# RWKV-5 attention and a tanh-shrink MLP on one core: the four loads of a w_in piece shared out over two queues by halves of partitions, with new costs in the planner

## The chip, the core and the metric

The kernel runs on one core of a Trainium2 chip. The core's engines work side by side, each through its own list of instructions in order: TensorE (PE; its weight loads are shown as PEld), VectorE (DVE), ScalarE (ACT), GpSimd (POOL) and SyncE (SP). SP and POOL here issue the DMAs; each is a queue of its own. The time is device microseconds per execution: 605.67 us in the median of three (603.26 to 606.02) before the change.

## What is computed

First a linear recurrence for 4 batches of 8 heads with 768 steps and 48 values per head, then an MLP over the 3072 tokens of 384 values that come out of it:

```python
for t in range(S):
    kt, vt, rt = (k[:, :, t], v[:, :, t], r[:, :, t])
    cur = np.einsum('bhd,bhe->bhde', u[None] * kt, vt)
    y[:, :, t] = np.einsum('bhd,bhde->bhe', rt, state + cur)
    state = w[None, :, :, None] * state + np.einsum('bhd,bhe->bhde', kt, vt)
x = y.transpose(0, 2, 1, 3).reshape(B * S, H * D)
h = x @ w_in                       # 384 x 2048
g = h - np.tanh(h)
return (g @ w_out).astype(np.float32)   # 2048 x 384
```

w_in and w_out arrive as float64, the rest as float32.

## The kernel before, in words

**The recurrence** is worked in 24 units of 64 steps for two batches each (`unit(n)`): batch half z = 0 lies in rows (partitions) 0 to 63, z = 1 in rows 64 to 127. A unit fetches r, k and v, each in two DMAs of 96 KB (`fetch`, line 750, all on SP), transposes r and k on PE (`turn`, line 763), forms levels, outputs and the state's update on PE (line 717), and leaves its result in `xt`. A third of the heads' rows goes through a tile `rest` and from there by six small DMAs on POOL, SBUF to SBUF, into rows 48 to 63 and 112 to 127 of `xt` (`fill`, line 876). Two units make one block of 256 tokens for the MLP.

**The MLP** takes a block and 256 columns of w_in at a time (`hidden`): `h` on PE (line 168), five activations on ACT (177 to 185), four operations on DVE (192 to 198), then `o` (line 206) or, in the last eight sixteenths, a scheme with seven products (line 257), for which POOL forms sums of g.

**The weights** come in 16 pieces, in the order of n: two of w_in, two of w_out, and so on. A piece is loaded as 64-bit words into a staging tile `st` and converted to float32 by five operations on DVE and two on ACT (`convert`, lines 137 to 143). A piece of w_out is one DMA to all 128 rows, on SP. A piece of w_in has four parts, because each head pair is padded to 64 rows: `parts[0]` goes to rows 0 to 47 (288 KB), `parts[1]` to rows 48 to 63 (96 KB), `parts[2]` to rows 64 to 111 (288 KB), `parts[3]` to rows 112 to 127 (96 KB). All are issued at line 123. Before the change SP issues parts 0 and 2 and POOL parts 1 and 3. The conversion waits for all four.

**The order of the instructions** is not written by hand. Every task is given to a planner (`Plan.add`) with its engine, a cost in us, what it waits for and, for a DMA, `data`, the time that it takes of a common channel. `Plan.forward` plays the tasks through; `Plan.order` shakes their due times at random, some thousands of times from a fixed seed, and keeps what is no worse. The order of the best play is the order in which the kernel's instructions are written, on each engine and each queue. `steps` counts PE instructions for code loading; LANDS, LANDED and SLOW are what a DMA takes to land; LANES limits the DMAs in flight of a queue to 8; a task marked `gated` (the weights) may not start over 45 us before it is due. In the planner before, a DMA from whatever queue waits only for the common channel:

```python
channel = max(channel, start + 1.2) + t.data
end = max(end + self.LANDS, channel + self.LANDED) + self.slow(start)
```

Of the kernel before, what the change touches and what calls it, by code (L numbers as in the profile page):

```python
# [33 lines left out]
AHEAD = 2  # L34
# [266 lines left out]
class Plan:  # L301
# [6 lines left out]

    HOP, NEAR_HOP, LANDS, LANDED, LANES, EARLY, SPARE, WARM, SLOW = 0.16, 0.06, 2.4, 1.6, 8, 45.0, 20.0, 6.0, (60.0, 3.0)
    AHEAD, BUSY = 0.05, 240.0  # L310
    CHUNK, CHUNK_0, ASKED, COMES, FIRST = 256, 192, 55, 3.4, 9.5
# [4 lines left out]

    def add(self, engine, cost, run, after=(), due=1e9, data=0, gated=False, steps=0):
        t = SimpleNamespace(engine=engine, cost=cost, run=run, after=[x for x in after if x], due=due, data=data,
                            gated=gated, steps=steps, then=[], n=len(self.tasks))
        for x in t.after:  # L320
            x.then.append(t)
        self.tasks.append(t)
        return t
# [12 lines left out]
    def forward(self, due, until=1e9):  # L336
# [3 lines left out]
        waiting = self.queues(ready, count)  # L340
        free, lanes, channel = dict(self.BEGIN), {}, 0.0
        step, bound, comes, fills = 0, self.CHUNK_0, 0.0, iter(self.fills)
# [3 lines left out]
        while len(done) < len(ready):  # L346
# [40 lines left out]
            if t.data:  # L387
                channel = max(channel, start + 1.2) + t.data
                end = max(end + self.LANDS, channel + self.LANDED) + self.slow(start)
                lanes[e] = lanes[e][1:] + [end]  # L390
# [58 lines left out]

    def order(self, first=2500, tries=500):  # L450


        due = [t.due for t in self.tasks]
        for t in reversed(self.tasks):
            for x in t.then:
                due[t.n] = min(due[t.n], due[x.n] - t.cost - self.HOP - (self.LANDS if t.data else 0))
        plan = self.forward(due)
        for _ in range(4):
            due = self.backward(plan)
            plan = self.forward(due)  # L460
        chance = Random(5)

        def moved():
            by, at, wide = chance.choice((0.3, 1, 2, 5)), chance.uniform(0, until), chance.choice((15, 40, 100, 700))
            return [x + chance.gauss(0, by) * (start is not None and abs(start - at) < wide / 2) for x, start in zip(due, plan[1])]


        until = self.BUSY
        plan = self.forward(due, until)
        for _ in range(first):  # L470
            new = moved()
            other = self.forward(new, until)
            if other[0] <= plan[0]:
                plan, due = other, new
        plan = self.forward(due)
        until = plan[0]
        for _ in range(tries):
            new = moved()
            other = self.forward(new)
            if chance.random() < .5:  # L480
                latest = self.backward(other)
                again = self.forward(latest)
                if again[0] < other[0]:
                    other, new = again, latest
            if other[0] <= plan[0]:
                plan, due = other, new
        self.due = due
        _, starts, done = plan
        self.forward(due)
        fitted, order = {n: (free, runs) for free, n, runs in self.fitted}, []  # L490
        for t in done:
            t.start = starts[t.n]
            free, runs = fitted.get(t.n, (0.0, [])) if t.engine == "PE" else (0.0, [])
            order += [SimpleNamespace(engine="PE", cost=0.0, start=free, run=run) for run in runs]
            order.append(t)
        return order
# [19 lines left out]
def near(ctx, tc, r, k, v, w, u, out, shared, moe_w_in, moe_w_out):  # L516
# [136 lines left out]
    def fills(to):  # L653
# [20 lines left out]
    doubled = add("ACT", .6, lambda: A.copy(twice, inverse[:, :, None, 1:].to_broadcast([128, NP, 2, SHORT])), [now])  # L674
    now = tabled = add("PE", .7, table, [doubled], steps=8)
    downs = add("ACT", .5, lambda: A.copy(w_down, tab.rearrange("s (h d) -> s h d", h=H)[:, :, :D]), [now])
# [6 lines left out]
        out=ub.rearrange("p h d -> p (h d)"),  # L683
        in_=bass.AP(tensor=u.tensor, offset=u.offset, ap=[[0, 128], [1, H * D]])), data=.7)

# [15 lines left out]
    for n in range(weights.count):  # L701

        queues, data = (("SP",), (3.0,)) if n % 4 > 1 else (("SP", "POOL") * 2, (1.2, .95) * 2)
        of = [add(e, .55, lambda n=n, i=i, e=e: weights.load(n, i, e_of[e]), [converted[n - 4] if n >= 4 else None],
                  data=x, gated=True) for i, (e, x) in enumerate(zip(queues, data))]
        if weights.sources[n % 4 > 1].dtype != I64:
            converted.append(of[-1])
            continue
        step = steps(lambda n=n: weights.convert(n))
        now = of + ([converted[n - 2]] if n >= 2 else [])  # L710
        for name, cost in (("DVE", .47), ("DVE", .47), ("ACT", .84), ("ACT", .84), ("DVE", .87), ("DVE", .87), ("DVE", .87)):
            now = [add(name, cost, step, now)]
        converted += now
# [7 lines left out]
    def unit(n):  # L721
# [21 lines left out]
        direct = j == 0  # L743

        def fetch(name, src, after):
            def run(z):
                if name == "k" and not hasattr(t, "kt"):
                    t.kt = first_k[slot] if direct else load.tile([128, H, D], F32, name="kt", tag="kt")
                to = {"r": rt, "v": vt}.get(name)
                Q.dma_start(out=(t.kt if to is None else to)[HALF[z], :, :D],  # L750
                            in_=src[half * 2 + z, :, steps_at, :].rearrange("h t d -> t h d"))

            of = [add("SP", .65, lambda z=z: run(z), after, data=.71) for z in range(2)]
            return add("none", 0, lambda: None, of)
# [135 lines left out]
        if two:  # L890
            free = [b1.xt, b1.rest, b1.add, b1.cp, b1.diag]
        turns, turned = .46, 16
        x.turn = add("PE", turns, lambda: turn(rt, r_ps), [x.r] + free, steps=turned)
# [9 lines left out]
        if product:  # L903
            now = add("ACT", 1.05, own_k, [x.kT, w_us])
            x.own = add("PE", .7, own_levels, [now, x.rT, b2.out], steps=64)
            x.diag = add("DVE", .64, lambda: V.copy_predicated(t.at, same.bitcast(I32)[:, None, None, :].to_broadcast([128, 2, NP, SHORT]), own_lev), [x.own, b2.out])
# [7 lines left out]
        if two:  # L914
            now = add("PE", .66, from_state, both + [x.rT, b1.xt, b1.rest, b1.add, b2.decay, x.kT], steps=64)
            begun = [add("ACT", .15, between, [now])]
        x.lev = add("PE", .7 if two else (1.33 if swap else 1.73) if ch else .7, levels,
                    begun + [x.kT, x.rT, b2.out] + ([b2.decay, b1.xt, b1.rest, b1.add] if ch else []), steps=128 if ch and not two else 64)
        x.cp = add("DVE", .64, lambda: V.copy_predicated(t.at, before, lev), [x.lev, b2.out] + ([] if product else [x.diag]))  # L919
        x.out = now = add("PE", .95 if direct else 1.21, outputs,  # L920
                          [x.cp, x.diag, x.v, b1.xt, b1.rest, b1.add] + ([x.extra] if direct else [x.kw]), steps=96 if direct else 128)
        if direct:
            now = x.out = add("PE", .55, to_state, [now, x.kw], steps=64)
        x.xt = add("ACT", .96 if swap else .4, to_xt, [now, last_h.get(j - FIRST - 2) if slot == 0 else None])
        if not direct:
            x.rest = add("ACT", .62 if swap else .26, to_rest, [x.xt] + (filled.get((j - 2, "all"), []) if slot == 0 else []))
        x.add = add("DVE" if ch else "ACT", .47 if ch else 1.2, keep, [x.out, x.rest, x.xt]) if more else None
        x.decay = x.add if not ch else add("DVE", .47, lambda: V.tensor_tensor(state[:, :, :, :D], state[:, :, :, :D], w_all, ALU.mult), [x.add]) if more else None
        if direct:
            filled.setdefault((j, "all"), []).append(x.xt)  # L930
        elif slot == L - 1:
            filled[j, "all"] = [add("POOL", .52, lambda i=i, kk=kk: fill(i, kk), [x.rest, x.xt], data=.1)
                                for kk in range(NK) for i in range(2)]
# [17 lines left out]
    def finished_seven(t, x, half, due, pace):  # L951
# [9 lines left out]
        for i in (1, 0):  # L961
            now = steps[4 if i else 6]
            if t.fs[0]:
                now = add("DVE", .47, lambda i=i: dense.gather(t, i), [now], due + 3 * pace)
            stored[j, i] = [add("POOL", .6, lambda z=z, i=i: dense.store(t.os[i], L * j + i, z, G), [now], due + 4 * pace, data=.4)
                            for z in range(2)]

    def hidden(j, fs, f, due, pace, seven=False):
# [40 lines left out]
        for i in range(L):  # L1009
# [7 lines left out]
            if whole and j < d.NB - 1:  # L1017

                stored[j, i] = [add("POOL", .6, lambda z=z, i=i, ends=ends: dense.store(ends.o, L * j + i, z, G),
                                    [x.empty[-1]], due + 4 * pace, data=.4) for z in range(2)]  # L1020

# [339 lines left out]
```

## Time and profile before

| | |
|---|---|
| median of three | 605.67 us |
| the profiled execution, its own time | 607.26 us |
| its span, first to last instruction | 605.5 us |
| PE / PEld busy | 582.4 / 485.7 us (96% / 80%) |
| DVE / ACT / POOL busy | 466.4 / 403.3 / 201.0 us |
| w_in loads on SP | 16, 288 KB each, 5.5 us from issue to landing (median) |
| w_in loads on POOL | 16, 96 KB each, 6.0 us |
| w_out loads on SP | 8, 768 KB each, 4.5 us |
| r, k, v loads on SP | 140, 96 KB each, 2.9 to 3.4 us |
| fills of xt on POOL | 66, 16 KB each, 2.1 us |

The page's rows of 40 slices of 15 us each show busy tenths; DMA is the mean busy share of the 16 DMA engines:

```profile
PE   8877999999999999999999999999999999999996
DVE  6699699999999999867677776767765775555666
POOL 5002212021000123544455473425334435334540
DMA  6966585967300210110111020122201100100101
```

Nearly all of the DMA work lies in the first ten slices, where the weights are loaded and 16 of the 24 units run. PE's row has its low digits in the first four slices. Busy PE includes filler matmuls (line 655) that the planner sets into holes before the first real work. A profile is one execution; sums are made against its own time.

### The profile page before, as it was taken

To read this page: it belongs to the slowest core of one execution; us is meant where nothing else is said; L and a number is where in the kernel's file an instruction comes from. 1 tells how busy PE (TensorE), PEld (TensorE's weight loads), DVE (VectorE), ACT (ScalarE), POOL (GpSimd) and SP (SyncE) were. 2 spreads that over 40 slices of the span, in tenths; PEclk is the share of its full clock that TensorE was granted. 3 is DMA by queue.
4 is the path that set the end of the run, shared out by engine and by line. 5 is a ranking of instruction groups with operands and counts; after the bars stand their busy time and mean duration, and the time that the engine had idled before them with its cause. 6 is when DMAs were issued, how large, how long until landed. Compare 5 with 4: busy or idle time off the path is not lost.

```text
span 605.5 us, 14670 instructions
## 1 busy us (share of the span) xinstructions
PE 582.4 (96%) x5781; PEld 485.7 (80%) x5781; DVE 466.4 (77%) x782; ACT 403.3 (67%) x902; POOL 201.0 (33%) x366
## 2 busy tenths in 40 slices
PE   8877999999999999999999999999999999999996
PEld 4555767667777669999999999888889889889995
DVE  6699699999999999867677776767765775555666
ACT  3677699899866676655556686465866676565652
POOL 5002212021000123544455473425334435334540
PEclk9889899999999999999999999999999999999999
DMA  6966585967300210110111020122201100100101
GB/s 125 228 126 126 113 194 99 143 167 124 105 14 0 48 28 14 26 27 1 28 27 26 2 60 1 41 41 48 53 16 34 41 2 8 29 2 8 26 3 30
DMA packets 86326, 33.78 MB, mean 56 GB/s; under 512 B 78536, under 2 KB 80680, under 8 KB 86248
## 3 DMA queue, kind: packets, MB, share of 16 engines
q1 hardware_dynamic: 81084, 25.57, 21.1%
q0 software_dynamic: 4992, 6.99, 5.5%
q8 instruction: 47, 0.77, 0.5%
q14 instruction: 31, 0.25, 0.2%
q10 hardware_dynamic: 172, 0.20, 0.1%
HBM read 26.94 MB, written 4.72 MB: 52 GB/s over the span
## 4 chain that ended last, share of the span: by engine, by line
PE 76%; DVE 6%; DMA 5%; ACT 4%; issue 4%; SPq 3%; POOL 1%; DVEq 0%; ACTq 0%; POOLq 0%
PE h L168 37%; PE p L257 26%; PE o L206 6%; PE yk_ps L717 4%; SPq L750 3%; DMA st<-in_moe_w_in_dram 2%; DMA xt<-rest 1%; PE yk_ps L763 1%; POOL xt L876 1%; DMA st<-in_moe_w_out_dram 1%; DVE rT L767 1%; DVE at L919 1%; ACT s L177 1%; DVE tg L194 1%; DVE g L198 1%
## 5 line engine op out<-in xcount | busy, mean ns | idle before, releaser
L168 PE MATMUL h<-xt,w_in_sb 128*128 128x256 f32 x1152 | 285.7, 385 | 2.7 <-DMA xt<-rest 2.7
L168 PEld LDWEIGHTS h<-xt,w_in_sb 128*128 128x128 f32 x1152 | 214.6, 192 | 35.9 <-issue 2.1
L242 POOL TENSOR_TENSOR sg<-g 128x256 f32<-128x256 f32 x69 | 52.1, 755 | 176.7 <-DVE g L198 152.2
L257 PE MATMUL p<-mixed,sg 128*128 128x192 f32 x426 | 104.1, 326 | 0.0
L192 DVE TENSOR_TENSOR g<-h,th 128x512 f32<-128x512 f32 x96 | 65.8, 686 | 48.9 <-ACT s L177 23.0
L194 DVE SCALAR_TENSOR_TENSOR tg<-s,tg 128x512 f32<-128x512 f32 x96 | 71.1, 741 | 36.6 <-ACT tg L181 20.0
L181 ACT ACTIVATE tg<-h 128x512 f32<-128x512 f32 x96 | 57.2, 596 | 58.5 <-PE h L168 56.9
L179 ACT ACTIVATE th<-h 128x512 f32<-128x512 f32 x96 | 57.4, 598 | 39.1 <-PE h L168 39.0
L177 ACT ACTIVATE s<-h 128x512 f32<-128x512 f32 x96 | 57.4, 598 | 37.3 <-PE h L168 37.2
L876 POOL DMA_DIRECT2D xt<-rest x66 | 32.5, 499 | 146.3 <-ACT rest L855 145.8
L257 PEld LDWEIGHTS p<-mixed,sg 128*128 128x128 f32 x426 | 75.0, 190 | 0.3 <-issue 0.3
L198 DVE COPY_PREDICATED g<-small,tg 128x512 f32<-128x512 int32 x96 | 71.1, 741 | 4.7 <-DVE tg L196 0.5
L257 PE MATMUL p<-w_out_sb,g 128*128 128x192 f32 x284 | 71.9, 335 | 1.1 <-DVE at L919 1.1
L196 DVE SCALAR_TENSOR_TENSOR tg<-q,tg 128x512 f32<-128x512 f32 x96 | 67.5, 703 | 6.4 <-ACT q L183 2.4
L206 PE MATMUL o<-w_out_sb,g 128*128 128x384 f32 x192 | 71.3, 495 | 0.1
L183 ACT ACTIVATE q<-s,m1b 128x512 f32<-128x512 f32 x96 | 69.8, 727 | 0.6
L185 ACT ACTIVATE small<-s,smallb 128x512 f32<-128x512 f32 x96 | 69.6, 725 | 0.3
L257 PEld LDWEIGHTS p<-w_out_sb,g 128*128 128x128 f32 x284 | 51.8, 190 | 9.0 <-DVE at L919 1.5
L788 ACT ACTIVATE at<-same,du 128x64 f32<-128x64 f32 x184 | 47.9, 343 | 2.8 <-DVE du L784 2.6
L206 PEld LDWEIGHTS o<-w_out_sb,g 128*128 128x128 f32 x192 | 35.2, 190 | 15.8 <-DVE g L198 0.2
L246 POOL TENSOR_TENSOR sg<-sg,g 128x128 f32<-128x128 f32 x69 | 41.0, 594 | 5.1
L244 POOL TENSOR_TENSOR sg<-sg,g 128x128 f32<-128x128 f32 x69 | 36.6, 530 | 5.2
(133 smaller groups left out, 672.3 us busy)
## 6 DMA issues: line engine op xcount, KB each, us to landing
st<-in_moe_w_out_dram SPq DMA_DIRECT2D x8, 768.0 KB, 4.5
rt<-in_r_dram SPq DMA_DIRECT2D x48, 96.0 KB, 2.9
vt<-in_v_dram SPq DMA_DIRECT2D x48, 96.0 KB, 3.4
st<-in_moe_w_in_dram SPq DMA_DIRECT2D x16, 288.0 KB, 5.5
kt<-in_k_dram SPq DMA_DIRECT2D x44, 96.0 KB, 3.1
out_dram<-o POOLq DMA_DIRECT2D x44, 96.0 KB, 2.2
st<-in_moe_w_in_dram POOLq DMA_DIRECT2D x16, 96.0 KB, 6.0
xt<-rest POOLq DMA_DIRECT2D x66, 16.0 KB, 2.1
```

What stands on the lines that cost most here:

```text
L168: self.nc.tensor.matmul(t.h2[:, z], self.w_in_sb[:, t.f // 2, kk, z * 128 : (z + 1) * 128], self.xts[t.j][:, kk].rearrange("p b t -> p (b ...
L177: A.activation(out, t.h, AF.Square)
L179: A.activation(out, t.h, AF.Tanh)
L181: A.activation(out, t.h, AF.Tanh, scale=G1)
L183: A.activation(out, t.s, AF.Square, bias=self.m1b)
L185: A.activation(out, t.s, AF.Relu, bias=self.smallb, scale=-1.0)
L192: V.tensor_tensor(t.g, t.h, t.th, ALU.subtract)
L194: V.scalar_tensor_tensor(t.tg, t.s, C4, t.tg, ALU.mult, ALU.mult)
L196: V.scalar_tensor_tensor(t.tg, t.q, K1, t.tg, ALU.add, ALU.mult)
L198: V.copy_predicated(t.g, t.small.bitcast(I32), t.tg)
L206: self.nc.tensor.matmul(self.outs[i], t.g2[:, z, i * C : (i + 1) * C], self.w_out_sb[:, t.f + z, :], start=t.first and z == 0, stop=t.last ...
L257: self.nc.tensor.matmul(ps[bank][:, half * n : (half + 1) * n], a, b, start=t.first and half == 0, stop=t.last, skip_group_check=True)
```

## The change

Two things change. The parts of a w_in piece keep their order, but the queues become SP, POOL, POOL, SP: SP has rows 0 to 47 and then 112 to 127, POOL has rows 48 to 63 and then 64 to 111. And the planner gets a time for each half of the rows (`ports`), a line for each queue (`ring`), a `side` for each DMA that goes to one half, and new costs; its search starts four times from the same point and looks at the first 110 us at first, where it looked at 240.

```diff
-    HOP, NEAR_HOP, LANDS, LANDED, LANES, EARLY, SPARE, WARM, SLOW = 0.16, 0.06, 2.4, 1.6, 8, 45.0, 20.0, 6.0, (60.0, 3.0)
-    AHEAD, BUSY = 0.05, 240.0
+    HOP, NEAR_HOP, LANDS, LANDED, LANES, EARLY, SPARE, WARM, SLOW = 0.16, 0.06, 2.1, 1.35, 8, 45.0, 20.0, 6.0, (60.0, 1.5)
+    AHEAD, BUSY, STARTS = 0.05, 110.0, 4
+    HALF = 1.75
...
             if t.data:
-                channel = max(channel, start + 1.2) + t.data
-                end = max(end + self.LANDS, channel + self.LANDED) + self.slow(start)
+
+                begin = max(start + 1.4, ring.get(e, 0.0))
+                channel = max(channel, begin) + t.data
+                ring[e] = channel
+                if t.side is not None:
+                    ports[t.side] = max(ports[t.side], begin) + self.HALF * t.data
+                    ring[e] = max(channel, ports[t.side])
+                end = max(end + self.LANDS, ring[e] + self.LANDED) + self.slow(start)
...
-    def order(self, first=2500, tries=500):
+    def order(self, first=2000, tries=300):
...
-        queues, data = (("SP",), (3.0,)) if n % 4 > 1 else (("SP", "POOL") * 2, (1.2, .95) * 2)
+        queues, data, sides = (("SP",), (2.5,), (None,)) if n % 4 > 1 else (("SP", "POOL", "POOL", "SP"), (.82, .4, .82, .4), (0, 0, 1, 1))
...
-            of = [add("SP", .65, lambda z=z: run(z), after, data=.71) for z in range(2)]
+            of = [add(queue(z), .65, lambda z=z: run(z), after, data=.28, side=z) for z in range(2)]
...
-        turns, turned = .46, 16
+        turns, turned = .38, 16
...
-        x.lev = add("PE", .7 if two else (1.33 if swap else 1.73) if ch else .7, levels,
+        x.lev = add("PE", .6 if two else (1.06 if swap else 1.46) if ch else .56, levels,
...
-        x.out = now = add("PE", .95 if direct else 1.21, outputs,
+        x.out = now = add("PE", .86 if direct else .97, outputs,
...
-            filled[j, "all"] = [add("POOL", .52, lambda i=i, kk=kk: fill(i, kk), [x.rest, x.xt], data=.1)
+            filled[j, "all"] = [add("POOL", .52, lambda i=i, kk=kk: fill(i, kk), [x.rest, x.xt], data=.1, side=i)
```

The new `queue(z)` returns "SP" for both halves as it stands, so r, k and v stay on SP. The loop with four starts in `order` and some smaller costs of the same kind (the table's transposes, own levels, the first state, the loads of u, the stores of the output) are left out above. No operation of the kernel's own work is added or removed.

More of the change, by code (lines that the diff above doesn't have):

```diff
@@ L315, in __init__, with add @@
         self.tasks, self.fills = [], []
-    def add(self, engine, cost, run, after=(), due=1e9, data=0, gated=False, steps=0):
+    def add(self, engine, cost, run, after=(), due=1e9, data=0, gated=False, steps=0, side=None):
         t = SimpleNamespace(engine=engine, cost=cost, run=run, after=[x for x in after if x], due=due, data=data,
-                            gated=gated, steps=steps, then=[], n=len(self.tasks))
+                            gated=gated, steps=steps, side=side, then=[], n=len(self.tasks))
         for x in t.after:
@@ L340, in forward @@
         waiting = self.queues(ready, count)
-        free, lanes, channel = dict(self.BEGIN), {}, 0.0
+        free, lanes, channel, ring, ports = dict(self.BEGIN), {}, 0.0, {}, [0.0, 0.0]
         step, bound, comes, fills = 0, self.CHUNK_0, 0.0, iter(self.fills)
@@ L465, in moved @@
             return [x + chance.gauss(0, by) * (start is not None and abs(start - at) < wide / 2) for x, start in zip(due, plan[1])]
[L468 to L474, printed above, removed]
+        until, begun, best = self.BUSY, due, None
+        for _ in range(self.STARTS):
+            due = begun
+            plan = self.forward(due, until)
+            for _ in range(first):
+                new = moved()
+                other = self.forward(new, until)
+                if other[0] <= plan[0]:
+                    plan, due = other, new
+            if best is None or plan[0] < best[0]:
+                best = plan[0], due
+        due = best[1]
         plan = self.forward(due)
@@ L674, in near @@
     doubled = add("ACT", .6, lambda: A.copy(twice, inverse[:, :, None, 1:].to_broadcast([128, NP, 2, SHORT])), [now])
-    now = tabled = add("PE", .7, table, [doubled], steps=8)
+    now = tabled = add("PE", .5, table, [doubled], steps=8)
     downs = add("ACT", .5, lambda: A.copy(w_down, tab.rearrange("s (h d) -> s h d", h=H)[:, :, :D]), [now])
@@ L683, in near @@
         out=ub.rearrange("p h d -> p (h d)"),
-        in_=bass.AP(tensor=u.tensor, offset=u.offset, ap=[[0, 128], [1, H * D]])), data=.7)
+        in_=bass.AP(tensor=u.tensor, offset=u.offset, ap=[[0, 128], [1, H * D]])), data=.5)
     add("ACT", 1.3, lambda: A.activation(fixed("warm", [128, 1]), shared["one"], AF.Tanh), due=0)
@@ L701, in near @@
     for n in range(weights.count):
-        queues, data = (("SP",), (3.0,)) if n % 4 > 1 else (("SP", "POOL") * 2, (1.2, .95) * 2)
+        queues, data, sides = (("SP",), (2.5,), (None,)) if n % 4 > 1 else (("SP", "POOL", "POOL", "SP"), (.82, .4, .82, .4), (0, 0, 1, 1))
         of = [add(e, .55, lambda n=n, i=i, e=e: weights.load(n, i, e_of[e]), [converted[n - 4] if n >= 4 else None],
-                  data=x, gated=True) for i, (e, x) in enumerate(zip(queues, data))]
+                  data=x, gated=True, side=side) for i, (e, x, side) in enumerate(zip(queues, data, sides))]
         if weights.sources[n % 4 > 1].dtype != I64:
@@ L743, in unit, with queue @@
         direct = j == 0
+        def queue(z):
+            return "SP" if not z else "ACT" if n < 0 else "POOL" if n < 0 else "SP"
         def fetch(name, src, after):
@@ L749, in run @@
                 to = {"r": rt, "v": vt}.get(name)
-                Q.dma_start(out=(t.kt if to is None else to)[HALF[z], :, :D],
+                e_of[queue(z)].dma_start(out=(t.kt if to is None else to)[HALF[z], :, :D],
                             in_=src[half * 2 + z, :, steps_at, :].rearrange("h t d -> t h d"))
-            of = [add("SP", .65, lambda z=z: run(z), after, data=.71) for z in range(2)]
+            of = [add(queue(z), .65, lambda z=z: run(z), after, data=.28, side=z) for z in range(2)]
             return add("none", 0, lambda: None, of)
@@ L903, in unit @@
         if product:
-            now = add("ACT", 1.05, own_k, [x.kT, w_us])
-            x.own = add("PE", .7, own_levels, [now, x.rT, b2.out], steps=64)
+            now = add("ACT", 1.2, own_k, [x.kT, w_us])
+            x.own = add("PE", .5, own_levels, [now, x.rT, b2.out], steps=64)
             x.diag = add("DVE", .64, lambda: V.copy_predicated(t.at, same.bitcast(I32)[:, None, None, :].to_broadcast([128, 2, NP, SHORT]), own_lev), [x.own, b2.out])
@@ L914, in unit @@
         if two:
-            now = add("PE", .66, from_state, both + [x.rT, b1.xt, b1.rest, b1.add, b2.decay, x.kT], steps=64)
+            now = add("PE", .58, from_state, both + [x.rT, b1.xt, b1.rest, b1.add, b2.decay, x.kT], steps=64)
             begun = [add("ACT", .15, between, [now])]
-        x.lev = add("PE", .7 if two else (1.33 if swap else 1.73) if ch else .7, levels,
+        x.lev = add("PE", .6 if two else (1.06 if swap else 1.46) if ch else .56, levels,
                     begun + [x.kT, x.rT, b2.out] + ([b2.decay, b1.xt, b1.rest, b1.add] if ch else []), steps=128 if ch and not two else 64)
         x.cp = add("DVE", .64, lambda: V.copy_predicated(t.at, before, lev), [x.lev, b2.out] + ([] if product else [x.diag]))
-        x.out = now = add("PE", .95 if direct else 1.21, outputs,
+        x.out = now = add("PE", .86 if direct else .97, outputs,
                           [x.cp, x.diag, x.v, b1.xt, b1.rest, b1.add] + ([x.extra] if direct else [x.kw]), steps=96 if direct else 128)
         if direct:
-            now = x.out = add("PE", .55, to_state, [now, x.kw], steps=64)
+            now = x.out = add("PE", .5, to_state, [now, x.kw], steps=64)
         x.xt = add("ACT", .96 if swap else .4, to_xt, [now, last_h.get(j - FIRST - 2) if slot == 0 else None])
@@ L926, in unit @@
             x.rest = add("ACT", .62 if swap else .26, to_rest, [x.xt] + (filled.get((j - 2, "all"), []) if slot == 0 else []))
-        x.add = add("DVE" if ch else "ACT", .47 if ch else 1.2, keep, [x.out, x.rest, x.xt]) if more else None
+        x.add = add("DVE" if ch else "ACT", .47 if ch else .95, keep, [x.out, x.rest, x.xt]) if more else None
         x.decay = x.add if not ch else add("DVE", .47, lambda: V.tensor_tensor(state[:, :, :, :D], state[:, :, :, :D], w_all, ALU.mult), [x.add]) if more else None
@@ L964, in finished_seven @@
                 now = add("DVE", .47, lambda i=i: dense.gather(t, i), [now], due + 3 * pace)
-            stored[j, i] = [add("POOL", .6, lambda z=z, i=i: dense.store(t.os[i], L * j + i, z, G), [now], due + 4 * pace, data=.4)
+            stored[j, i] = [add("POOL", .6, lambda z=z, i=i: dense.store(t.os[i], L * j + i, z, G), [now], due + 4 * pace, data=.3)
                             for z in range(2)]
@@ L1019, in hidden @@
                 stored[j, i] = [add("POOL", .6, lambda z=z, i=i, ends=ends: dense.store(ends.o, L * j + i, z, G),
-                                    [x.empty[-1]], due + 4 * pace, data=.4) for z in range(2)]
+                                    [x.empty[-1]], due + 4 * pace, data=.3) for z in range(2)]
     for n in range(L * (FIRST + 2)):
```

## The prediction

> **What bounds the kernel now.** I read the table of stretches first, because the page's 96% for TensorE is an average. Columns: stretch, its length, busy us and count of PE, PE's weight loads, DVE, ACT, POOL, granted PE clock, DMA share, GB/s.
>
> ```profile
> 15.00:35.00 20.00, 17.05 (x267) 10.33 (x271) 14.54 (x25) 14.00 (x37) 0.57 (x1) 0.91 0.93 199
> 35.00:55.00 20.00, 15.56 (x365) 11.61 (x355) 19.77 (x36) 16.14 (x50) 3.94 (x8) 0.91 0.68 128
> 55.00:70.00 15.00, 11.96 (x178) 8.56 (x181) 9.73 (x18) 7.38 (x24) 0.76 (x2) 0.77 0.52 93
> 70.00:80.00 10.00, 10.00 (x229) 7.04 (x222) 9.20 (x18) 9.64 (x32) 3.52 (x7) 1.00 1.01 216
> 80.00:90.00 10.00, 9.19 (x169) 6.63 (x167) 9.11 (x16) 9.01 (x22) 2.98 (x6) 1.00 0.76 170
> 90.00:120.00 30.00, 28.12 (x564) 20.70 (x564) 28.58 (x50) 26.52 (x73) 4.93 (x10) 1.00 0.79 125
> 120.00:135.00 15.00, 13.80 (x189) 9.29 (x188) 15.00 (x26) 13.91 (x35) 3.27 (x6) 1.00 0.64 165
> 135.00:200.00 65.00, 65.00 (x380) 47.96 (x379) 64.09 (x103) 51.66 (x96) 2.06 (x4) 1.00 0.27 59
> 200.00:590.00 390.00, 388.72 (x3228) 347.35 (x3227) 277.63 (x460) 245.99 (x524) 170.11 (x287) 1.00 0.12 25
> ```
>
> From 135 us PE has no holes: 65.00 of 65 and 388.72 of 390. The change adds no matmul there, so the end moves only by how much earlier the kernel arrives at this state. Up to there DVE is the full engine: it converts the weights, serves the recurrence and makes the activations. Its idle time between 15 and 135 us is 5.46 + 0.23 + 5.27 + 0.80 + 0.89 + 1.42 + 0.00 = **14.1 us**. I take that as the purse: a us of it saved is a us off the end, provided PE can follow, and PE has 2.95 + 4.44 + 3.04 + 0.81 + 1.88 + 1.20 = 14.3 us of holes in the same stretches, plus filler matmuls. It holds two large sums, one in 15 to 35 and one in 55 to 70.
>
> Next the chain that ended last (start us, us, what) and, below it, two rows of the timeline and two stretches, to see what these sums wait for.
>
> ```profile
> 10.94 8.65 DMA st<-in_moe_w_in_dram
> 27.13 3.43 SPq L750
> 34.97 2.36 DMA kt<-in_k_dram
> 52.54 6.17 DMA xt<-rest
> 101.73 4.46 DMA st<-in_moe_w_in_dram
> ```
>
> ```profile
> 19.71 0.56 DVE L137 TENSOR_SCALAR power<-st 128x768 uint32<-128x768 uint32 x1 [2.91 <-DMA st<-in_moe_w_in_dram]
> 56.98 0.67 PE L168 MATMUL h<-xt,w_in_sb 128*128 128x256 f32 x2 [1.55 <-DMA xt<-rest]
> ```
>
> ```profile
> 16.00:19.00 3.00, 1.83 (x35) 1.04 (x35) 0.80 (x2) 2.31 (x10) 0.00 (x0) 1.00 1.19 159
> 25.00:28.00 3.00, 3.00 (x19) 2.22 (x18) 2.33 (x5) 0.54 (x2) 0.00 (x0) 0.95 1.03 400
> ```
>
> The reader is to see: the chain runs through DMAs five times, twice for w_in itself; DVE stands 2.91 us for the first w_in piece; and the DMA engines are full in both of the last two rows, yet move 159 GB/s when w_in, r, k and v are on the way (each to rows of one half) and 400 GB/s when w_out is (all 128 rows). So what w_in pays for is not bytes; it is where they go.
>
> **The change, part by part.**
>
> *The four loads of a w_in piece.* Still four DMAs, 288 + 96 + 288 + 96 KB, still two on SP and two on POOL. Only the second 288 KB and the last 96 KB change places. Before, SP moved rows 0 to 47 and then 64 to 111, 576 KB in a line; POOL's 96 KB parts were done early. Now each queue moves 384 KB, and while SP fills rows 0 to 47, POOL, once past its 96 KB, fills rows 64 to 111. In 13 to 19 us the DMA view gives a mean of 165 GB/s, so 768 KB take 768 / 165 = 4.65 us of the channel. Side by side it is 384 / 165 = 2.33 us: **2.3 us** less.
> No row of this trace shows two large loads to different halves at once, so the price needs both ends. The lower is a rule that speaks against the change: the Trainium skill's page "SBUF — State Buffer", section "Can I just issue two DMAs to hit both halves?", says that two concurrent DMAs, one at partition 0 and one at 64, gain 6% and serialize. That would be 0.06 x 4.65 = 0.3 us per piece. The upper end is the w_out row: 768 / 400 = 1.92 us, a gain of 2.7. I take 2.3: the page's test doesn't say that the two came from different queues, and here the engines are full at 159 GB/s with far more to give, which looks like packets waiting for one side.
>
> *First piece.* DVE waits 2.91 us for it at 19.71; 2.3 of that goes. Next in line are the levels of unit 1 on PE (18.14 plus 0.45) and unit 1's v, which frees POOL at 20.29; no more than 2.9 can go. **-2.3** (ends -0.3 and -2.9).
>
> *SP's queue behind it.* r, k and v stay on SP; they now have 192 KB less in front per piece, 192 / 165 = 1.2 us. The chain stands 3.43 us in SP's queue at 27.13 and waits for k at 34.97. DVE's idle time from 25 to 36 is 0.67 + 0.90 + 0.25 = 1.8 us by its stretches, which caps it; I take half, **-1.0** (ends 0 and -1.8).
>
> *The fills of xt* (SBUF to SBUF, six on POOL per block) land 2.1 us after issue in the median, but 6.17 in the one on the chain: it is issued at 52.54, with SP's w_in load of 51.65 and k in flight and POOL's two w_in loads right behind. PE stands 2.7 us for it in two waits, loses its clock (0.77 in 55 to 70), and DVE idles 5.27 us. A piece that clears 2.3 us sooner should give most of this wait back: **-2.0**. The lower end is a loss: a 288 KB load now stands in POOL's own line, and a fill issued just behind it waits 288 / 165 = 1.75 us more (+1.75). The upper end is the whole 5.27.
>
> *POOL's issue.* 96 KB cost it 524 ns, 16 KB 486; going on in a line, 288 KB cost about 0.62 us. POOL was busy 0.57 of the 20 us from 15 to 35 and 3.94 of the next 20: nothing waits, 0. Were that cover gone, 8 x 0.1 us. Here the same page has a second warning ("The 'DVE blocks DMA' trap"): a GpSimd DMA beside a two-port DVE operation went from 620 to 3100 ns. The row: the slowest POOL issue of w_in, beside L137 at 73 us, took 836 ns, against 524. By the row eight more heavy issues cost 8 x 0.3 us of POOL's idle time; by the page 8 x 2.5 us, partly ahead of fills. I follow the row: 0.
>
> *The planner's costs.* All matmul groups of the units become cheaper on paper (turn 0.46 to 0.38; outputs 1.21 to 0.97), landing too (2.4 to 2.1; the surcharge after 60 us 3.0 to 1.5), r/k/v 0.71 to 0.28 of the channel, and halves get a time of their own; the search has four starts and looks at 110 us, not 240. No instruction is added; only the order on each queue changes, everywhere. Against the timeline's rows: eight transposes take 0.39 us from start to the next group's start (6.26 to 6.65), outputs and state update of one unit 0.95 (34.38 to 35.33), so the new numbers for PE are the nearer ones; a 96 KB r load lands 2.9 us after issue in the median, which neither hits. What a new order is worth the trace can't say; its ends are the rest of the purse (14.1 - 5.7 = 8.4 us gained) and a stall like the one at 55 us made anew (5.3 lost). For the small stalls from 70 to 120 us (3.1 us of DVE idle time), I take **-0.4**; for the rest 0. After 135 us a different order of full work costs nothing.
>
> **Sum:** -2.3 - 1.0 - 2.0 - 0.4 = -5.7 us. The profiled execution took 607.26 (span 605.5 and 1.8 around it), so it would take 601.6; it lies 1.6 above the median of 605.67, so the forecast is 605.67 - 5.7 = **600.0 us**.
>
> **Rivals.** What this measurement can tell from no change is about 0.5%: 602.6 to 608.7.
>
> *The halves serialize* (the +6%). Then the first piece gives 0.3, SP's queue maybe 0.5, the fills nothing, order 0.4: -1.2, 604.5. For it: the rule, and DMA share above 0.9 in both rows. Against: 400 GB/s with the same engines.
>
> *The purse is opened wider.* The new costs of landing and halves let the planner keep fills and weights apart, both large stalls go (2.9 + 1.8 + 5.27) and half a us of the small ones: -10.5, 595.2. For it: these stalls are all DMA, which is what the planner's model is told anew. Against: DVE must be given other work in just those places.
>
> *POOL's line* (slower). If the 288 KB load stands ahead of the six fills of a block, each such block costs 1.75 us in the line and then the clock: in the stretch around 61 us six matmuls of h took 2.85 us against 1.29 later, 1.6 more. That is 3.35 a place. The first two parts still give 3.3, so one place brings it to even, and two bring +3.4, **609.1**; it decides from the second on. For it: POOL issues fills and w_in back to back at 50, 69 and 101 us. Against: fills stood ahead of the w_in loads in each of these, and the planner now counts the line.
>
> *The change doesn't do what it says:* the four loads could be issued so far apart that no two halves meet, as when SP is blocked. Then it is like the first rival; its chance is inside it.
>
> **How the numbers follow.** Forecast 0.50 (597 to 602.5 nearly throughout), wider purse 0.21, serialized 0.16, POOL's line 0.11, the rest 0.02. Faster: 0.48 + 0.21 + 0.06 = 0.75. Within: 0.02 + 0.10 + 0.01 = 0.13. Slower: 0.12. The range 595.0 to 606.5 takes the forecast, over half of the wider purse and all but the upper edge of the serialized case, about 0.8. The likeliest one's own is 597 to 602.5.
>
> **What would show it.** (1) The first w_in piece lands within 7 us of its first SP load, not 8.65 after its second, and DVE's wait at L137 is under 1 us; if GB/s stays near 165 while rows 0 to 47 and 64 to 111 are both in flight, the +6% rule is right. (2) DVE idles under 10 us from 15 to 135. (3) Fills that leave beside w_in land in under 4 us; if they land in 6 or more behind a POOL load, it is POOL's line. (4) The DMA view has 16 w_in issues on each queue as before, with other sizes. (5) PE stays full from some 129 us on. Wrong from the ground it would be if the time changes with the stretch after 135 us, which I hold to be fixed.

## The result, and the profile after

The changed kernel takes **599.79 us** in the median of eight runs (599.01 to 602.89), beside 605.39 for the kernel before on the same chip; the ratio is 0.9908, interval 0.9886 to 0.9929. The profiled execution took 600.11 us with a span of 598.4, 7.1 less than before. The forecast of 600.0 is met, but by luck in the sum: of its four terms the three for the loads, 5.3 us together, show up nowhere in the time, and the smallest, 0.4 us for the order, carries the gain.

The table of stretches of the changed kernel, with the columns and bounds of the one before (stretch, length, busy us and count of PE, PEld, DVE, ACT, POOL, PE clock, DMA share, GB/s):

```profile
15.00:35.00 20.00, 13.90 (x322) 10.10 (x310) 13.31 (x22) 13.74 (x40) 0.27 (x1) 0.83 0.94 188
35.00:55.00 20.00, 17.07 (x334) 11.61 (x333) 19.07 (x36) 16.75 (x50) 5.54 (x10) 1.00 0.83 142
55.00:70.00 15.00, 13.48 (x306) 9.47 (x306) 12.49 (x22) 12.08 (x35) 2.94 (x6) 1.00 0.99 158
70.00:80.00 10.00, 10.00 (x186) 7.68 (x185) 8.95 (x17) 7.01 (x24) 0.00 (x0) 1.00 0.74 173
80.00:90.00 10.00, 9.87 (x174) 6.84 (x176) 9.81 (x19) 9.44 (x27) 2.86 (x6) 1.00 0.80 190
90.00:120.00 30.00, 29.94 (x570) 21.70 (x570) 28.64 (x50) 28.66 (x74) 8.74 (x16) 1.00 0.61 108
120.00:135.00 15.00, 14.45 (x57) 10.90 (x58) 14.92 (x24) 10.96 (x22) 0.00 (x0) 1.00 0.46 135
135.00:200.00 65.00, 65.00 (x444) 47.43 (x443) 63.51 (x102) 52.08 (x98) 2.18 (x4) 1.00 0.25 59
200.00:590.00 390.00, 387.92 (x3238) 348.54 (x3237) 280.32 (x466) 246.94 (x528) 169.20 (x287) 1.00 0.12 25
```

The reader is to see: from 15 to 35 us, where the weights come in, it is worse than before (DVE 13.31 us busy against 14.54, PE 13.90 against 17.05, PE's clock 0.83 against 0.91, and no more GB/s). From 35 us to 135 PE is at least as busy as before in every row, and its clock is 1.00 where it had been 0.91 and 0.77. DVE is busier in 55 to 70 and 80 to 90 and about as busy as before in the other rows. DVE's idle time from 15 to 135 us is 6.69 + 0.93 + 2.51 + 1.05 + 0.19 + 1.36 + 0.08 = 12.8 us, against 14.1. Only 1.3 us came out of the purse that the forecast was counted from, and the end of the profiled execution moved by 7.1.

The first w_in piece in the changed kernel's timeline:

```profile
18.22 0.56 DVE L137 TENSOR_SCALAR power<-st 128x768 uint32<-128x768 uint32 x1 [2.72 <-DMA st<-in_moe_w_in_dram]
22.07 0.69 PE L729 MATMUL x_ps<-rT,kT 48*64 48x64 f32 x13 [2.08 <-issue]
29.88 1.32 PE L168 MATMUL h<-xt,w_in_sb 128*128 128x256 f32 x5
```

DVE still stands 2.72 us for it. PE then loses 2.08 us in the middle of a group of levels with no wait that the profile shows ("issue"; what it is was not found), and the first h starts at 29.88, where it started at 25.51 before. The chain of the changed kernel has no fewer DMA steps in its first 100 us: five, and a stand of 3.32 us in SP's queue, where the chain before had four and one of 3.43.

```profile
13.80 3.32 SPq L766
17.16 6.22 DMA rt<-in_r_dram
31.41 3.52 DMA kt<-in_k_dram
48.30 5.38 DMA xt<-rest
82.45 4.96 DMA xt<-rest
99.25 4.63 DMA st<-in_moe_w_in_dram
```

**Where the time came from.** How many h matmuls (line 168) begin in a stretch shows how far the MLP is. Two rows of the kernel before, then two of the changed one (stretch, length, busy us and count of PE and PEld, clock, DMA share, GB/s):

```profile
0.00:60.00 60.00, 9.33 (x30) 6.41 (x30) 0.94 0.78 151
60.00:135.00 75.00, 24.95 (x95) 18.36 (x96) 0.96 0.73 144
```

```profile
0.00:60.00 60.00, 8.95 (x36) 6.51 (x36) 0.94 0.86 158
60.00:135.00 75.00, 29.35 (x120) 22.39 (x120) 1.00 0.66 139
```

Up to 60 us the two are level (six h more, but four o matmuls, line 206, fewer). From 60 to 135 the changed kernel does 120 h instead of 95. By 135 us it has 31 h and 9 o more: 31 x 0.215 + 9 x 0.37 = 10.0 us of full PE work ahead (six h take 1.29 us in the chain, four o 1.49). A small part of this is an exchange: of the recurrence's matmuls and transposes it has 1808 done by then, before it was 1880; that is some 1.4 us, an estimate from the chain, where 32 of these matmuls take 0.47 to 0.65 us and 16 transposes 0.65. From 135 us on PE is busy 456.4 us where it was 464.6, and idle 7.0 us where it was 6.0: 8.1 less and 1.0 more make the 7.1 of the end.

What DVE finishes in 60 to 135 us, again two rows of the kernel before and then two of the changed one: all engines, and the last operation on a tile of g alone (line 198: DVE, clock, DMA share, GB/s):

```profile
60.00:135.00 75.00, 70.81 (x1297) 51.04 (x1290) 67.23 (x116) 64.16 (x173) 15.47 (x30) 0.96 0.73 144
60.00:135.00 75.00, 5.83 (x8) 0.96 0.73 144
```

```profile
60.00:135.00 75.00, 72.73 (x1139) 52.93 (x1136) 70.46 (x122) 63.85 (x167) 14.54 (x28) 1.00 0.66 139
60.00:135.00 75.00, 8.04 (x11) 1.00 0.66 139
```

DVE is busy 70.46 us against 67.23 and finishes 11 tiles of g instead of 8: more DVE time, and more of it for tiles that feed PE.

### The profile page after: what moved, and what is told of

Same layout as the page of the kernel before. It is cut to its first block, busy times and chain, and to the rows that moved or that the text cites. A ratio compares the mean times of both kernels' runs of the same rounds, so it can differ in the third digit from the quotient of the medians.

```text
span 598.4 us, 14645 instructions
## 1 busy us (share of the span) xinstructions
PE 577.7 (97%) x5783; PEld 483.7 (81%) x5783; DVE 464.8 (78%) x782; ACT 402.3 (67%) x902; POOL 200.7 (34%) x366
## 4 chain that ended last, share of the span: by engine, by line
PE 78%; DVE 8%; DMA 4%; ACT 4%; SPq 3%; issue 2%; POOL 1%; DVEq 0%; POOLq 0%
PE h L168 37%; PE p L257 25%; PE o L206 8%; PE yk_ps L729 5%; SPq L766 2%; DMA xt<-rest 2%; DVE tg L196 1%; DMA rt<-in_r_dram 1%; PE yk_ps L779 1%; DVE mixed L266 1%; DVE g L198 1%; DVE g L192 1%; DMA st<-in_moe_w_in_dram 1%; DVE rT L783 1%; POOL xt L892 1%
## 5 line engine op out<-in xcount | busy, mean ns | idle before, releaser
L168 PE MATMUL h<-xt,w_in_sb 128*128 128x256 f32 x1152 | 281.9, 382 | 1.4 <-DMA xt<-rest 1.2
L194 DVE SCALAR_TENSOR_TENSOR tg<-s,tg 128x512 f32<-128x512 f32 x96 | 68.7, 716 | 27.4 <-ACT tg L181 19.1
L246 POOL TENSOR_TENSOR sg<-sg,g 128x128 f32<-128x128 f32 x69 | 40.1, 581 | 4.9
L244 POOL TENSOR_TENSOR sg<-sg,g 128x128 f32<-128x128 f32 x69 | 36.1, 523 | 5.1
```

Of the source, the lines that this page charges most:

```text
L168: self.nc.tensor.matmul(t.h2[:, z], self.w_in_sb[:, t.f // 2, kk, z * 128 : (z + 1) * 128], self.xts[t.j][:, kk].rearrange("p b t -> p (b ...
L194: V.scalar_tensor_tensor(t.tg, t.s, C4, t.tg, ALU.mult, ALU.mult)
```

## The experiments

**Is it the queues or the order?** The planner runs anew for any edit, so two kernels keep one plan's order task by task and change only the queue that issues a part. In the changed kernel:

```diff
-        of = [add(e, .55, lambda n=n, i=i, e=e: weights.load(n, i, e_of[e]), [converted[n - 4] if n >= 4 else None],
+        of = [add(e, .55, lambda n=n, i=i, e=e: weights.load(n, i, e_of[e if n % 4 > 1 else ("SP", "POOL")[i % 2]]), [converted[n - 4] if n >= 4 else None],
```

and in the kernel before the same line with `("SP", "POOL", "POOL", "SP")[i]`.

> The changed kernel with its order of tasks kept task by task, but the four loads of each w_in piece issued as before: SP rows 0 and 64, POOL rows 48 and 112. Theory A (the gain is the planner's order alone; halves filled at once bring nothing): within 2 us of the changed kernel, 598 to 602 us. Theory B (the halves at once carry the first 2 to 5 us of the gain, as I predicted): 602 to 605 us, and the first piece lands over 1.5 us later than in the changed kernel.

> The kernel before with its order kept task by task, but the loads shared out as in the change: SP rows 0 and 112, POOL rows 48 and 64. Theory A: 604 to 607 us, no change, the first piece lands within 1 us of 19.6. Theory B: 601 to 603.5 us, DVE's wait of 2.9 us for the first piece falls below 1. Theory C (POOL's load shuts SP's small packets out): over 606 us, and r, k, v land over a us later than before in 10 to 20 us.

The runs come from several chips, on which the kernel before has medians from 605.4 to 606.8 us, so they are compared by their ratio to it. New order with the old queues: 0.9918 (0.9890 to 0.9945), where the changed kernel has 0.9908. Old order with the new queues: 1.0017 (0.9995 to 1.0039). The stretch from 60 to 135 us, first of old order with new queues, then of new order with old queues:

```profile
60.00:135.00 75.00, 70.61 (x1309) 50.49 (x1310) 68.20 (x119) 65.11 (x176) 15.67 (x30) 0.98 0.79 146
```

```profile
60.00:135.00 75.00, 71.87 (x1127) 52.08 (x1126) 69.50 (x120) 63.37 (x165) 14.48 (x28) 1.00 0.67 139
```

By the count of PE instructions and the clock each is the kernel whose order it has (before x1297, changed x1139), not the one whose queues it has. So the gain is the order's. Sharing the loads out is worth 0.1% in the new order and costs 0.2% in the old one, both within the noise; the 5.3 us, 0.9%, that I had given to the loads are excluded. On the first piece it acts both ways. DVE's wait for it, from the waits of the same two runs (total us, times, longest):

```profile
DVE power L137 <- DMA st<-in_moe_w_in_dram: 2.4, 1, 2.4
```

```profile
DVE power L137 <- DMA st<-in_moe_w_in_dram: 1.5, 1, 1.5
```

In the old order the new queues shorten it from 2.9 to 2.4; in the new order they lengthen it from 1.5 to 2.7. There DVE takes the piece up at 18.22 us with the new queues and at 17.39 with the old ones; Theory B had it over 1.5 us later with the old ones. What landed when, of the loads issued from 9 to 20 us: three rows of the kernel before, then four of its order with the new queues (count, KB each, median us from issue to landing):

```profile
vt<-in_v_dram SPq DMA_DIRECT2D x2, 96.0 KB, 5.2
rt<-in_r_dram SPq DMA_DIRECT2D x2, 96.0 KB, 8.2
kt<-in_k_dram SPq DMA_DIRECT2D x2, 96.0 KB, 7.9
```

```profile
st<-in_moe_w_in_dram SPq DMA_DIRECT2D x1, 288.0 KB, 8.3
vt<-in_v_dram SPq DMA_DIRECT2D x2, 96.0 KB, 4.4
rt<-in_r_dram SPq DMA_DIRECT2D x2, 96.0 KB, 9.3
kt<-in_k_dram SPq DMA_DIRECT2D x2, 96.0 KB, 8.8
```

r and k land 1.1 and 0.9 us later, v 0.8 earlier: Theory C's sign for two of three, at about its size. The first of the four rows is the load of rows 0 to 47. Before, it landed after 6.0 us, and rows 64 to 111 came last, after 8.65; now rows 64 to 111 come first, from POOL, 6.1 us after issue, and rows 0 to 47 last, after 8.3. The halves have changed places, and the later of them comes hardly sooner.

**What do the halves give by themselves?** A kernel of loads alone, in stages that wait for each other, with the kernel's own patterns of w_in, w_out and r (one execution of it; one stage is shown, cut):

```diff
+    def stage_2():
+        for slot in range(4):
+            w_half(Q, slot, 0)
+            w_half(G, slot, 1)
```

> Only loads, in stages of about 2.3 MB that wait for each other; nothing of the reference is computed, the output is zeros. Rows of one half alone from SP: near 165 GB/s as in the kernel's stretch, 13 to 14 us a stage. Theory B: one half from SP beside the other half from POOL runs at 300 GB/s or more (under 8 us), and so does ACT in POOL's place; both from the same half stay near 165. Theory A (the rule of 6%): under 200 GB/s in all of these, 400 only for w_out's 128 rows. Beside r on SP, POOL's loads keep their rate and r's packets fall under half of theirs if Theory C holds.

One row per stage (bounds, length, busy us and count of DVE and POOL, clock, DMA share, GB/s; the length is the result, waits and landing included):

```profile
16.90:34.70 17.80, 0.00 (x0) 0.00 (x0) 1.00 0.89 133
53.50:70.00 16.50, 0.23 (x3) 0.00 (x0) 1.00 0.89 143
70.40:85.00 14.60, 0.20 (x3) 2.42 (x4) 1.00 0.85 162
85.40:103.50 18.10, 0.20 (x3) 2.28 (x4) 1.00 0.87 130
122.70:135.50 12.80, 0.14 (x2) 0.00 (x0) 1.00 0.84 184
135.90:144.20 8.30, 0.19 (x2) 0.00 (x0) 1.00 0.76 284
177.10:198.70 21.60, 0.22 (x2) 0.00 (x0) 1.00 0.99 146
199.20:220.60 21.40, 0.25 (x2) 2.28 (x4) 1.00 1.08 165
```

The first six move 2304 KB each. Rows 0 to 47 from SP alone: 17.8 us. Rows 0 and 64 in turn on SP: 16.5. SP rows 0 beside POOL rows 64, the change's way: **14.6**. Both queues to the same half: 18.1. ACT in POOL's place: 12.8. w_out to 128 rows: 8.3. The last two move r (768 KB, in 96 KB loads) and w_in (2304 KB) together: all on SP 21.6 us, SP and POOL by halves **21.4**. This last length also holds the start of the output's stores, which SP issues from 214.6 us on: the row's 165 GB/s are 3.53 MB, 0.38 more than in the row above. But in the first 15.3 us of each of the two stages, before any store, both moved 2.35 MB, 154 GB/s.

So the halves do run side by side from two queues: 18% less time than rows 0 to 47 alone with POOL and 28% with ACT, 12% and 22% less than with both halves on SP, as the kernel before had them. That is far from the doubling that Theory B wants. In rates it is 22% and 39% more than one half alone. The Trainium skill's page "SBUF — State Buffer", section "Can I just issue two DMAs to hit both halves?", has 6% for two loads at once and says that issuing from several engines doesn't help either: here both halves on SP gain 8%, and the second queue more, so the measurement decides. Once r's small packets are among them, which is the kernel's state at 10 to 20 us, these two stages show no gain left. Missed in what was expected: one half alone took 17.8 us, not 13 to 14, and w_out reached 284 GB/s over its stage, not 400. (The 197 and 225 GB/s of the next expectation come out as 2304 KB over 12.0 and 10.5 us, the loads' time from issue to landing; over whole stages it is 162 and 184.)

A further stage shows what the small packets suffer. While POOL fills rows 64 to 111 and SP loads r, from 164 to 171 us, the queues move (packets, MB, share of 16 engines):

```profile
q0 software_dynamic: 304, 0.95, 83.7%
q1 hardware_dynamic: 1056, 0.20, 29.8%
```

r gets 0.20 MB in 7 us, 29 GB/s; alone it moved at 112 in the 7 us from 154 to 161. POOL's load moves 0.95 MB in the 7 us, 136 GB/s; alone it moved at 137 (from 104.8 to 122 us). That this is also what holds r and k back in the kernel fits their landing times, but was not tried by itself.

**Is there a faster door for the second half?** In the changed kernel, order kept, rows 64 to 111 go to ACT:

> The changed kernel with its order of tasks kept; only rows 64 to 111 of each w_in piece are issued by ACT in POOL's place (eight more issues of about 0.46 us on ACT). By themselves SP and ACT fill the two halves at 225 GB/s where SP and POOL reach 197. If the rate at which the halves are filled decides anything here, it gains 1 to 2 us: 598 to 600.5 where the changed kernel is at 600 to 601. If the loads don't matter (as the kernel with the old queues shows), it is the same within 1.5 us or, by ACT's issues and waits, up to 3 us slower.

0.9938 (0.9916 to 0.9961), no better than the changed kernel and by its middle 0.3% worse; what ACT gains by itself doesn't reach the end.

**Is the order a lucky draw?** The planner's seed, in both kernels:

```diff
-        chance = Random(5)
+        chance = Random(6)
```

> The kernel before with another seed for the planner's random search: nothing but the order changes. Theory D (the change's gain is the draw of an order): this lies up to 6 us to either side of 605.5, as far from before as the change is. Theory E (the planner's new costs and search carry it): within 2.5 us of 605.5.

> As the one with seed 6. Theory D: anywhere from 598 to 612 us. Theory E: 603 to 608 us.

> The changed kernel with another seed. Theory D: scatters as widely as the old planner's seeds do and its mean is no lower than theirs. Theory E: 598 to 602.5 us, under both of the old planner's seeds.

> As the changed kernel with seed 6. Theory D: scatters from 598 to 610 us. Theory E: 598 to 602.5 us.

Old planner: 1 (seed 5), 0.9961 (0.9940 to 0.9982), 0.9985 (0.9959 to 1.0011). New planner: 0.9908 (seed 5), 0.9928 (0.9896 to 0.9959), 0.9902 (0.9870 to 0.9934). All three new draws lie under all three old ones: the draw is worth up to 0.4% within a planner, the planner's change some 0.7% between the means (0.9913 against 0.9982). This speaks for Theory E, but not for certain: with three draws each, mere chance would part them so once in twenty times, and the intervals of the two with seed 6 overlap.

**Which part of the planner?** Four kernels: the kernel before with the nine new costs of PE and ACT tasks alone; the kernel before with the new search alone; the changed kernel with the old search and the old nine costs, so that the DMA side alone is new (with the new queues); and the changed kernel with the old nine costs.

> The kernel before; only the nine costs of PE and ACT tasks are those of the change (turn 0.38, levels, outputs 0.97 and so on). Theory F (the engine costs carry the gain): 598 to 602.5 us. Theory G (the DMA side of the planner carries it: landing times, the surcharge after 60 us, shares of the channel, halves): 603.5 to 607 us. Theory H (the longer search does): 603.5 to 607 us.

> The kernel before; only the search is that of the change (four starts, the first 110 us, fewer tries). Theory H: 598 to 602.5 us. Theories F and G: 603.5 to 607 us, inside the spread that the old planner's seeds show (604.1 to 605.9).

> The changed kernel with the old search and the old nine engine costs: of the planner only the DMA side is new. Theory G: 598 to 602.5 us. Theories F and H: 603.5 to 607 us.

> The changed kernel with the old nine engine costs. Theory F: 603.5 to 607 us. Theories G and H: 598 to 602.5 us. If the three add up, it lies between.

In this order: 0.9976 (0.9956 to 0.9996), 0.9952 (0.9918 to 0.9987), 0.9928 (0.9882 to 0.9974), 0.9977 (0.9941 to 1.0013); of 605.39 us that is 603.9, 602.5, 601.0 and 604.0. The DMA side alone does the most, which speaks for Theory G; but the last kernel has it too, and the new search besides, and gains almost nothing. With draws of 0.4% and one draw for each part, these four don't settle it; which part of the planner carries the gain stays open.

What they share with all the others is the state at 135 us. h matmuls begun by then and span: before 125 and 605.5; old order with new queues 125, 605.9; old seeds 130 and 138, 605.0 and 604.6; search alone 131, 604.3; engine costs alone 140, 603.5; without the engine costs 140, 605.3; new seed 6 144, 601.5; ACT 146, 602.3; DMA side alone 150, 600.8; new order with old queues 155, 598.8; changed 156, 598.4; new seed 7 156, 599.3. From one end to the other 31 h go with 7.1 us, 0.23 us each, about the 0.215 us that an h takes: whoever has more of the MLP begun when PE becomes full ends earlier, by about that much. It is a trend of single executions, not a law: the two with 140 h lie 1.8 us apart.

## Why the prediction was right, and where it was wrong

*The bound* was right: in all of these kernels PE has next to no holes after 135 us (at least 64.8 of 65 us busy, then 387.7 to 389.4 of 390), and the time is set by how much work is left when it gets there. *The purse* was wrong as a measure. Idle time of DVE fell by 1.3 us and the end by 7.1, because a busy DVE isn't a usefully busy one: the changed order has DVE finish three more tiles of g in 60 to 135 us (12 instead of 10 by then) and convert no more than before (eight pieces by 135 us in both). Counted on PE over the whole span: its busy time fell from 582.4 to 577.7 us with the same work (h alone from 285.7 to 281.9, with the clock at 1.00 instead of 0.96 in 60 to 135) and its holes from 23.1 to 20.7; 4.7 + 2.4 = 7.1.

*First piece, -2.3.* This step failed. DVE's wait went from 2.91 to 2.72 us, and with the queues alone changed to 2.4 in the old order and from 1.5 to 2.7 in the new. I took two halves at once to run at 165 GB/s each, and SP's two loads, which it issues 0.66 us apart, to run one behind the other before; by themselves they save 12% against both halves on SP, an estimated 0.5 us of 4.65, and beside r's loads about nothing. The low end was the right one, not for the reason that the rule gives (alone, they do overlap): r, k and v are in flight beside them, which is the likely reason. I also passed over that the section I cited says of several issuing engines that they don't help. The first h came 4.4 us later, but that is the order's doing: with the old queues in the new order it starts at 30.43.

*SP's queue, -1.0.* Wrong in sign, or nothing: 192 KB less in front, yet r and k landed 1.1 and 0.9 us later with the order kept. The term's own measure, DVE's idle time from 25 to 36 us, went from 1.8 to 3.7 us by the queues alone in the old order and stayed at 0.9 in the new one. The stage with r beside POOL's load shows the likely reason: I priced the line and left out the neighbour.

*The fills, -2.0.* The stretch is right, its cause is not. DVE's idle time in 55 to 70 us fell from 5.27 to 2.51 and PE's waits for fills from 2.7 to 1.2; but new order with old queues is just as busy there (DVE 12.59 us against 12.49), and PE waits only 0.5 us for fills, so the order did it, not a faster piece. In the old order the queues alone did bring the idle time to 3.70, but PE waited 2.5 us for the fills as before, 15 to 35 us lost about as much (DVE 13.25 us busy against 14.54), and the end stood still. The fill on the chain still takes 5.38 us.

*The planner, -0.4.* This is the term that was mis-sized: 605.39 x (1 - 0.9918) = 5.0 us of the 5.6 come with the order alone. I gave the order ends of 8.4 us gained and 5.3 lost and took a value near nothing, because no row of a trace shows what a plan not yet made is worth.

*POOL's issue, 0.* Right: 582 ns in the median for both sizes together, against 523, and at most 972; the 3100 ns of the page's second warning didn't appear.

*The rivals:* POOL's line didn't appear; the fills stand ahead of the loads, with 2.4 us in the median at 47 to 49 us. The serialized case was near in what the loads are worth, next to nothing, but had 0.4 us for the order. The wider purse had the planner as its cause, but the purse itself hardly opened.

*The signs* told it before the experiments did. DVE took up the first piece 9.0 us after its first SP load, not within 7, and its wait stayed far over 1 us; it idled 12.8 us from 15 to 135, not under 10; the fills on the chain took 5.38 and 4.96 us, not under 4. Only the 16 issues on each queue and the full PE from 129 us on came as forecast, and PE was nearly full there before too (5.95 of 6 us).

So the number was right by luck: 5.3 us that the loads didn't bring were made good by 5.0 us of the order that I had at 0.4. The worse first 35 us come with the new order too (with the old queues PE and DVE are busy 13.88 and 13.68 us there), and the order makes them good later. The total could not tell this; the two kernels with orders kept did.

## What to carry to other kernels

Where a planner writes the order, an edit to its costs is an edit to the whole kernel: keep the order and change only the operation to learn what the operation is worth, and change only the seed to learn what a draw is worth, before a gain is given to either. Count the work done by the time the engine that bounds the kernel fills up, not the idle time of the engine that feeds it. Before transfers are split over queues, ask what small packets of others they will run beside.

## What the runs showed of the hardware that was not expected

Two halves of the rows filled from two queues take 18% less time from SP and POOL and 28% less from SP and ACT than one half alone (17.8 us to 14.6 and 12.8 for 2304 KB), while w_out in loads to 128 rows takes 8.3: the halves neither serialize nor add up. Why ACT's queue does better than POOL's was not tried. And a queue of 192-byte runs beside one of large loads doesn't share evenly: SP's r fell from 112 to 29 GB/s beside POOL's w_in, which lost nothing (136 GB/s, and 137 alone). All of this is one execution of one kernel of loads.
